# Merging the preparation products of a DeltaNet recurrence into the recurrence's own visits of TensorE

## The chip, the cores and the metric

The kernel runs on one core of a Trainium2 chip. The metric is device time in microseconds (us); the time of a kernel is the median of several executions. A profile shows one execution, with the engines named PE (TensorE's matmuls), PEld (TensorE's weight loads), DVE (VectorE), ACT (ScalarE), POOL (GpSimd) and SP (SyncE, which here only issues DMAs).

## The reference

Two blocks follow each other, in float32. The first is a DeltaNet layer over 4 batches, 8 heads, 768 positions and head dimension 48:

```
k_n = k / (norm(k) + 1e-06)
for t in range(S):
    y[t]  = q[t] @ state
    v_old = state^T k_n[t]
    state = state + beta[t] * outer(k_n[t], v[t] - v_old)
```

The second takes y as 3072 tokens of width 384 (8 heads x 48) through a gated FFN of width 1536:

```
out = (silu(x @ w_gate) * (x @ w_val)) @ w_out
```

## The kernel before

**Chunks.** The sequence is cut into 12 chunks of 64 positions. A chunk of all 32 batch-heads gives 256 tokens, which are one unit of the FFN. The FFN of chunk c (called FFN c here) carries the recurrence of chunk c+1 inside it.

**The FFN.** `gate_val` (L840) computes two of the twelve 128-wide slices of the hidden layer: the gate product, then the value product (`p_gate` and `p_val`, L847), each in one bank of a four-bank rotation in PSUM that `ps_ffn` (L74) hands out. ACT applies Silu, and DVE multiplies into `h_f` (L862). Six such gate pairs make an FFN. From FFN 3 on `output_fast` (L950) does the second product with seven small products per 2x2 split instead of eight; for this the last three gate pairs also form sums of h on DVE (`sums_of_h`, L942), and the output adds up on DVE (L969).

**The recurrence.** `advance(c)` (L730) is a generator of four steps: first v minus what the state predicts (`p_r`, and with it `p_y`, the state's share of y); then `p_u`, which applies the chunk's inverse `zt`; then the new state (`p_s`) and the rest of y (`p_y`, L782); then the transposes (`p_f`, L827) that make `x_ffn`, the input of the next FFN. Its products are 64x64, 32 of them in a group.

**What a chunk needs beforehand.** `turned` (L410) turns k and q of a chunk. From chunk 6 (k) and 3 (q) on it is one DVE instruction each (L422) out of blocks that were loaded by eight DMAs, and it issues the loads of the next chunk's blocks on SP. `gram` (L470) makes the k-k and the q-k products (L444); DVE copies the first (L467) and masks the second (L459). For each pair of chunks, `invert(g)` (L641) solves for the inverse on DVE: turns, a square root by a power on POOL (L655), then 31 steps of two instructions each (`substitute`, L505), and turns again. `join(g)` (L696) then completes the inverse with two groups of 32x32 products on TensorE (L706 and L720), with ACT between them.

**The order of the work.** All five engines' queues are filled in the order of the program text. Two helpers spread the recurrence over the FFN. `point(c+1)` (L1091) stands at nine places of an FFN from FFN 3 on: before each of the six gate pairs, before the output, and twice in it (L984 and L991). Such a place is called a visit here, numbered 0 to 8; the word is also used for the group of small products that TensorE then does between the FFN's products. A point does one thing: the next step of `advance` if it has begun; else one piece of preparation, by `prep_step` (L1064): half a join, or `turned`, or both Gram products of `products` (L1029); else the first step of `advance`. `finish` (L1099) at an FFN's end does what is left. `fill(n)` (L1110) puts the next n pieces of the inverse on DVE: two and three in each gate pair, then 2, 2 and 7 in the output, the 7 at its end (L1003). Where a piece waits for POOL, it says so and the fill is cut short.

**PSUM.** Eight banks: four for the FFN, and two pairs with the tags `px` and `py`, which the recurrence and its preparation share. A tile of a tag waits until the one before it in that tag has been read.

Of the kernel before, what the change touches and what calls it, by code (L numbers as in the profile page):

```python
# [11 lines left out]
ALU = mybir.AluOpType  # L12
# [9 lines left out]
def kernel(  # L22
# [25 lines left out]
    nc = tc.nc  # L48
# [21 lines left out]
    def ps_pair(name, tag):  # L70

        return psum.tile([128, 2, 512], FP32, name=name, tag=tag, bufs=1)

    def ps_ffn(shape, name):  # L74
        return psum.tile(shape, FP32, name=name, tag="ffn", bufs=4)
# [261 lines left out]
    def every():  # L337
        for bp in range(NB):
            for j in range(NJ):
                for n, (par, b) in enumerate(ORDER):  # L340
                    yield bp, j, par, b, bp == 0 and j == 0
# [128 lines left out]
    def gram(*args):  # L470
        for _ in gram_steps(*args):
            pass
# [100 lines left out]
    def recur(p, m=D):  # L573
        p = p[:, :, 0 : NB * NJ * m]
        return p.rearrange("p x (bp j d) -> p x bp j d", bp=NB, j=NJ)
# [120 lines left out]
    def join(g):  # L696

        zt, a, z1 = ztp[g % ZB], a_sb[g], z1s[g]
        M = HH // 2
        p_j = ps_pair("p_j", "px")[:, 0].rearrange("p (c m i) -> p c m i", c=2, m=M)  # L700
        for c in range(2):
            for m in range(M):
                for e in range(2):
                    for s in range(2):
                        dst, lo = QUADS[2 * s + e][0], QUADS[2 * s + 1][0]
                        nc.tensor.matmul(  # L706
                            p_j[dst, c, m],
                            a[lo, c, 2 * m + e, 0:R],
                            zt[lo, c, 2 * m + e, R:C],
                        )  # L710
        t2 = work.tile([128, 2, M, R], FP32, name="t2", tag="tmp", bufs=1)
        nc.scalar.mul(t2, p_j, -1.0)
        yield
        p_j = ps_pair("p_j", "py").rearrange("p e (c m i) -> p e c m i", c=2, m=M)
        for c in range(2):
            for m in range(M):
                for e in range(2):
                    for s in range(2):
                        row, hi = QUADS[2 * s + e][0], QUADS[2 * s][0]
                        nc.tensor.matmul(p_j[hi, e, c, m], z1[row, c, m], t2[row, c, m])  # L720
        zt_v = zt.rearrange("p c (m e) i -> p e c m i", e=2)
        for s, copy in ((0, nc.scalar.copy), (1, nc.vector.tensor_copy)):
            hi = QUADS[2 * s][0]
            copy(
                zt_v[hi, :, :, :, R:C].rearrange("p e c m i -> p e (c m) i"),
                p_j[hi].rearrange("p e c m i -> p e (c m) i"),
            )
        yield

    def advance(c):  # L730

        kn = knp[slot(c)]
        zt = ztp[c // 2 % ZB][:, c % 2]
        zt = zt.rearrange("p (par bp j) i -> p par bp j i", par=2, bp=NB)
        if c > 0:
            scale_v(c)
        r = vin.pop(c)
        p_y = recur(ps_pair("p_y", "py"))
        if c > 0:
            p_r = recur(ps_pair("p_r", "px"))  # L740
            for bp, j, par, b, first in every():
                nc.tensor.matmul(  # L742
                    p_r[half_of(b ^ par), par, bp, j],
                    kt[c][half_of(par), bp, j, b],
                    state[half_of(par), b, bp, j],
                    start=first,
                    stop=True,
                    skip_group_check=True,
                )
            for bp, j, par, b, first in every():  # L750
                nc.tensor.matmul(  # L751
                    p_y[half_of(b ^ par), par, bp, j],
                    qt[c][half_of(par), bp, j, b],
                    state[half_of(par), b, bp, j],
                    start=first,
                    stop=False,
                    skip_group_check=True,
                )
            nc.vector.tensor_tensor(out=r, in0=r, in1=p_r, op=ALU.subtract)  # L759
        yield  # L760
        p_u = recur(ps_pair("p_u", "px"))
        for bp, j, par, b, first in every():
            nc.tensor.matmul(  # L763
                p_u[half_of(b), par, bp, j],
                zt[half_of(b ^ par), par, bp, j],
                r[half_of(b ^ par), par, bp, j],
                start=first,
                stop=True,
                skip_group_check=True,
            )  # L770
        uu = work.tile([128, 2, NB, NJ, D], FP32, name="uu", tag="r", bufs=2)
        each = range(NB) if c == 0 else (slice(0, NB),)
        for bp in each:
            nc.scalar.copy(uu[:, :, bp], p_u[:, :, bp])
        if c + 2 < NCH:
            load_v(c + 2)
        yield
        pq = p_sb.pop(c)

        def p_of_u():  # L780
            for bp, j, par, b, first in every():
                nc.tensor.matmul(  # L782
                    p_y[half_of(b ^ par), par, bp, j],
                    pq[half_of(b), par, bp, j],
                    uu[half_of(b), par, bp, j],
                    start=(c == 0 and first),
                    stop=True,
                    skip_group_check=True,
                )

        def of_state():
            p_s = recur(ps_pair("p_s", "px"))
            for bp, j, par, b, first in every():
                nc.tensor.matmul(  # L794
                    p_s[half_of(par), b, bp, j],
                    kn[half_of(b), bp, 2 * j + par],
                    uu[half_of(b), par, bp, j],
                    start=first,
                    stop=True,
                    skip_group_check=True,  # L800
                )
            if c > 0:
                nc.vector.tensor_tensor(out=state, in0=state, in1=p_s, op=ALU.add)
            else:
                nc.scalar.copy(state, p_s)
            for later in range(AHEAD, NCH):
                if freed_by_k(later) == c:
                    load_k(later)

        if 0 < c < NCH - 1:  # L810
            of_state()
        p_of_u()
        y = work.tile([128, NB, NJ, 2, D], FP32, name="y", tag="r", bufs=2)
        for bp in each:
            nc.scalar.copy(y[:, bp, :, 0], p_y[:, 0, bp])
            for b in range(2):
                nc.scalar.copy(y[half_of(b), bp, :, 1], p_y[half_of(1 - b), 1, bp])
        yield

        y_f = y.rearrange("p bp j par d -> p bp (j par d)")  # L820
        xts[c] = ffn_pool.tile([128, KT, TOK], FP32, name="x_ffn")
        p_f = ps_pair("p_f", "py")[:, :, 0 : KT * 128]
        p_f = p_f.rearrange("p bp (t n) -> p t bp n", t=KT)
        for bp in range(NB):
            for t in range(KT):
                at = slice(t * 128, (t + 1) * 128)
                nc.tensor.transpose(p_f[:, t, bp], y_f[:, bp, at], ident)  # L827
        x_v = xts[c].rearrange("p t (bp n) -> p t bp n", bp=NB)
        for bp in each:
            nc.scalar.copy(x_v[:, :, bp], p_f[:, :, bp])  # L830
        yield
        if c == 0:
            of_state()
            yield
# [181 lines left out]
    def step(kind, fn, *args):  # L1016
        key = (kind, args or (1,))
        if key not in gens:
            gens[key] = [fn(*args), 0]
        next(gens[key][0], None)  # L1020
        gens[key][1] += 1

    def steps(kind, *args):
        return gens.get((kind, args), (None, 0))[1]

    fills = []
# [32 lines left out]
    def may_advance(c):  # L1059
        g = c // 2  # L1060
        due = {0: 1, 1: 2 + 2 * (c % 2)}.get(g, 2)
        return steps("advance", c) > 0 or (c in p_sb and steps("join", g) >= due)

    def prep_step(c):  # L1064
# [23 lines left out]
        going.append(gen)  # L1088
        return True

    def point(c):  # L1091

        mine = c < NCH and steps("advance", c) < 4 and may_advance(c)
        if mine and steps("advance", c) > 0:
            step("advance", advance, c)
        elif not prep_step(c - 1) and mine:
            step("advance", advance, c)

    def finish(c):  # L1099

        if c < NCH:
            while not may_advance(c):
                fill_some(1000)
                prep_step(c - 1)
            while steps("advance", c) < 4:
                step("advance", advance, c)
# [190 lines left out]
```

## Time and profile before

| what | value |
|---|---|
| median of 8 runs | 738.55 us (738.05 to 740.39) |
| profiled execution, its own time | 738.55 us |
| span of the profile | 736.8 us |
| PE busy | 699.2 us, 95% |
| DVE busy | 473.1 us, 64% |
| ACT, POOL busy | 154.7 and 67.8 us |

TensorE's first products of each FFN start at these times; a visit that stands before gate pair 0 is counted to its FFN:

| FFN | 3 | 4 | 5 | 6 | 7 | 8 | 9 | 10 | 11 |
|---|---|---|---|---|---|---|---|---|---|
| start, us | 249.63 | 304.83 | 361.88 | 415.88 | 472.93 | 526.93 | 582.53 | 636.54 | 687.88 |
| busy DVE, us | 24.2 | 46.7 | 27.9 | 46.7 | 27.8 | 44.4 | 26.9 | 13.8 | 11.1 |

The inverse of a pair of chunks runs mostly in the FFNs 4, 6 and 8, and ends in the one after.

How to read the profile's lines: a row of the order of time gives the start, the length, the engine, the line of the program, the operation, the tile written and those read, the count of merged instructions, and in brackets how long the engine had been idle and what released it. A float32 matmul leaves two records, so a gate product of six matmuls is x12, and a group of 32 small products is x64. Records of matmuls overlap, since they are pipelined; the distance between starts is what TensorE takes. A row of the waits gives who waited for whom: us in total, times, the longest.

### The profile page before, as it was taken

What the parts mean: (1) busy time and instruction counts of PE and PEld (TensorE: products, weight loads), DVE (VectorE), ACT (ScalarE), POOL (GpSimd) and SP (SyncE); (2) the same over time, 40 slices, a digit from 0 to 9 for tenths busy, and PEclk for the clock granted to TensorE, in tenths of its full rate; (3) what the DMA queues carried; (4) which work ended last, traced back from release to release, by engine and by line L of the source; (5) the groups of instructions that cost most, each with busy time, mean ns of one, the idle gap of its engine ahead of it and who ended that gap; (6) DMA issues with size and microseconds to landing.
All of it is one profiled execution on the core that took longest, in us unless ns stands there. A gap on an engine that the chain in (4) does not pass through costs nothing.

```text
span 736.8 us, 22478 instructions
## 1 busy us (share of the span) xinstructions
PE 699.2 (95%) x10132; PEld 605.8 (82%) x10132; DVE 473.1 (64%) x977; ACT 154.7 (21%) x287; POOL 67.8 (9%) x46
## 2 busy tenths in 40 slices
PE   4657999999999999999999999999999999999997
PEld 3545788866787788988988988988988988989987
DVE  6999988888498163678853678854678853313122
ACT  3555443302401112021012011012011012021010
POOL 7009100202100000030000030000030000000000
PEclk9957999999999999999999999999999999999999
DMA  7775343221231112330302331302211100100000
GB/s 147 185 227 150 114 109 129 40 37 24 57 45 24 23 24 45 44 67 12 54 3 46 43 64 21 51 3 41 45 28 14 31 3 3 23 3 0 22 1 21
DMA packets 130735, 37.18 MB, mean 50 GB/s; under 512 B 122864, under 2 KB 125936, under 8 KB 130640
## 3 DMA queue, kind: packets, MB, share of 16 engines
q1 hardware_dynamic: 127184, 34.01, 22.4%
q10 hardware_dynamic: 3072, 1.57, 1.0%
q8 instruction: 79, 1.29, 0.7%
q0 software_dynamic: 384, 0.17, 0.1%
q14 instruction: 16, 0.13, 0.1%
HBM read 31.01 MB, written 4.72 MB: 48 GB/s over the span
## 4 chain that ended last, share of the span: by engine, by line
PE 80%; DVE 15%; issue 2%; DMA 1%; ACT 1%; SPq 0%; DVEq 0%; ACTq 0%
PE p_gate L847 24%; PE p_val L847 23%; PE p_o L959 14%; PE p_o L876 6%; DVE tmp L510 3%; DVE zb L516 3%; PE p_g L444 2%; PE p_u L763 2%; PE p_r L742 1%; PE p_s L794 1%; PE p_y L782 1%; PE p_y L751 1%; DVE h_f L917 1%; DVE h_f L862 1%; PE p_j L630 1%
## 5 line engine op out<-in xcount | busy, mean ns | idle before, releaser
L847 PE MATMUL p_gate<-x_ffn,wg_sb 128*128 128x256 f32 x864 | 206.3, 389 | 1.5 <-ACT x_ffn L830 1.5
L847 PE MATMUL p_val<-x_ffn,wv_sb 128*128 128x256 f32 x864 | 198.5, 379 | 0.0
L847 PEld LDWEIGHTS p_gate<-x_ffn,wg_sb 128*128 128x128 f32 x864 | 162.4, 193 | 24.8 <-ACT x_ffn L830 2.0
L847 PEld LDWEIGHTS p_val<-x_ffn,wv_sb 128*128 128x128 f32 x864 | 163.8, 190 | 22.3
L862 DVE TENSOR_TENSOR h_f<-sil,p_val 128x512 f32<-128x512 f32 x71 | 48.6, 684 | 147.7 <-PE p_val L847 147.1
L856 ACT ACTIVATE sil<-p_gate 128x512 f32<-128x512 f32 x72 | 43.0, 598 | 278.4 <-PE p_gate L847 252.6
L655 POOL TENSOR_TENSOR n_b<-mb,half 128x32 f32<-128x32 f32 x5 | 43.9, 8772 | 407.7 <-DVE mb L480 368.2
L959 PE MATMUL p_o<-wo_sb,h_f 128*128 128x192 f32 x432 | 75.6, 328 | 0.1
L959 PEld LDWEIGHTS p_o<-wo_sb,h_f 128*128 128x128 f32 x432 | 70.3, 190 | 1.2 <-DVE o_sb L969 0.7
L510 DVE TENSOR_TENSOR tmp<-zb,mb 128x31 f32<-128x31 f32 (+15 forms) x186 | 63.3, 340 | 12.1 <-PE p_j L630 6.8
L516 DVE TENSOR_TENSOR zb<-zb,tmp 128x31 f32<-128x31 f32 (+15 forms) x186 | 63.7, 343 | 6.6 <-DVE tmp L510 0.2
L969 DVE TENSOR_TENSOR o_sb<-o_sb,p_o 128x192 f32<-128x192 f32 x45 | 15.7, 350 | 53.4 <-PE p_o L959 36.2
L876 PE MATMUL p_o<-wo_sb,h_f 128*128 128x384 f32 x136 | 45.7, 490 | 0.0
L876 PEld LDWEIGHTS p_o<-wo_sb,h_f 128*128 128x128 f32 x136 | 25.4, 190 | 16.5
L959 PE MATMUL p_o<-last_k,h_f 128*128 128x192 f32 x180 | 32.2, 326 | 0.0
L959 PEld LDWEIGHTS p_o<-last_k,h_f 128*128 128x128 f32 x180 | 29.7, 190 | 0.0
L917 DVE TENSOR_TENSOR h_f<-h_f,h_f 128x256 f32<-128x256 f32 x54 | 22.4, 424 | 8.0 <-PE p_o L959 7.1
L959 PE MATMUL p_o<-last_h,h_f 128*128 128x192 f32 x144 | 26.3, 326 | 0.0
L959 PEld LDWEIGHTS p_o<-last_h,h_f 128*128 128x128 f32 x144 | 23.9, 190 | 0.0
L254 ACT ACTIVATE last_h<-last_h,rebias 128x512 int32<-128x512 uint32 (+2 forms) x26 | 15.3, 615 | 28.7 <-DVE last_h L246 28.7
L763 PEld LDWEIGHTS p_u<-vin,zt 64*64 64x64 f32 x768 | 13.7, 141 | 6.4 <-issue 3.2
L763 PE MATMUL p_u<-vin,zt 64*64 64x48 f32 x768 | 15.7, 228 | 1.8 <-DVE vin L759 0.7
(180 smaller groups left out, 691.6 us busy)
## 6 DMA issues: line engine op xcount, KB each, us to landing
vin<-in_v_dram SPq DMA_DIRECT2D x96, 48.0 KB
kn<-in_k_dram SPq DMA_DIRECT2D x40, 96.0 KB
out_dram<-o_sb SPq DMA_DIRECT2D x36, 96.0 KB
zt<-in_moe_w_out_dram SPq DMA_DIRECT2D x6, 384.0 KB
staged<-in_moe_w_out_dram SPq DMA_DIRECT2D x6, 384.0 KB
qpad<-in_q_dram SPq DMA_DIRECT2D x36, 64.0 KB
wo_sb<-in_moe_w_gate_dram SPq DMA_DIRECT2D x4, 512.0 KB
wo_sb<-in_moe_w_val_dram SPq DMA_DIRECT2D x4, 512.0 KB
```

The costliest lines, as they stand in the source:

```text
L254: nc.scalar.activation(power.bitcast(I32), power, ACTF.Relu, bias=rebias, scale=8.0)
L510: nc.vector.tensor_tensor(out=t_v, in0=zb[:, 0 : j + 1, j : j + 1].to_broadcast([128, j + 1, m]), in1=mb[:, j : j + 1, j + 1 : R].to_broad ...
L516: nc.vector.tensor_tensor(out=zb[:, 0 : j + 1, j + 1 : R], in0=zb[:, 0 : j + 1, j + 1 : R], in1=t_v, op=ALU.add,)
L655: nc.gpsimd.tensor_tensor(out=n, in0=mb.rearrange("p j i -> p (j i)")[:, 0 : R * R : R + 1], in1=half, op=ALU.pow,)
L763: nc.tensor.matmul(p_u[half_of(b), par, bp, j], zt[half_of(b ^ par), par, bp, j], r[half_of(b ^ par), par, bp, j], start=first, stop=True, ...
L847: nc.tensor.matmul(ps[name][:, i], w_sb[:, t, (f + i) * 128 : (f + i + 1) * 128], xts[c][:, t], start=(t == 0), stop=(t == KT - 1),)
L856: nc.scalar.activation(sil, ps[name], ACTF.Silu)
L862: nc.vector.tensor_tensor(out=hs[c, f], in0=sil, in1=ps["p_val"], op=ALU.mult)
L876: nc.tensor.matmul(p_o, hs[c, f - f % 2][:, f % 2, bp * 128 : (bp + 1) * 128], wo_sb[:, f], start=(f == 0), stop=(f == FT - 1),)
L917: nc.vector.tensor_tensor(out=out, in0=a, in1=b, op=ALU.subtract)
L959: nc.tensor.matmul(p[x, part], a(f - f % 2)[:, f % 2], b(f), start=not begun and f == 0, stop=f == FH - 1, skip_group_check=True,)
L969: nc.vector.tensor_tensor(out=out, in0=a, in1=b, op=ALU.add)
```

## The change

From FFN 3 on (`point(c)` with c > 3) a new function `merged(c)` takes the place of the old rule. It has stages: 0 turns k (if one is free to be turned) and q; 1 does `advance`'s first step and one Gram product (that of k for an odd chunk that has one, else that of q); 2 does, for an even chunk, the first half of the join and the k Gram, and waits (doing nothing) until a visit earlier than its own has seen the inverse as ended; for an odd chunk with a k Gram it does the q Gram, and an odd chunk without one skips it; 3, for even chunks, does the second half of the join; 4, 5 and 6 do the other three steps of `advance`. `finish` runs the stages that are left.

In `advance` the product `p_y` of the state moves from the first step to the second, ahead of `p_u`; this holds for the chunks 1 to 3 too. In `join` the first `p_j` takes a bank of the FFN's rotation in place of the pair `px`.

```diff
@@ join
-        p_j = ps_pair("p_j", "px")[:, 0].rearrange("p (c m i) -> p c m i", c=2, m=M)
+        p_j = ps_ffn([128, 512], "p_j").rearrange("p (c m i) -> p c m i", c=2, m=M)
@@ advance
-        p_y = recur(ps_pair("p_y", "py"))
         if c > 0:
             p_r = recur(ps_pair("p_r", "px"))
             for bp, j, par, b, first in every():
...
+            nc.vector.tensor_tensor(out=r, in0=r, in1=p_r, op=ALU.subtract)
+        yield
+        p_y = recur(ps_pair("p_y", "py"))
+        if c > 0:
             for bp, j, par, b, first in every():
                 nc.tensor.matmul(
                     p_y[half_of(b ^ par), par, bp, j],
...
-            nc.vector.tensor_tensor(out=r, in0=r, in1=p_r, op=ALU.subtract)
-        yield
         p_u = recur(ps_pair("p_u", "px"))
@@ new
+    stage_of, seen = {}, set()
+
+    def merged(c):
+        if c >= NCH:
+            return
+        at, k_c, q_c = stage_of.get(c, (0, None, None))
+        g = c // 2
+        ready = c % 2 == 1 or g in seen
+        seen.update(inverted)
+
+        def a_step():
+            step("advance", advance, c)
+
+        def gram_k(tag):
+            if k_c is not None:
+                gram(k_c, False, tag, (nc.vector.tensor_copy,) * 2)
+                if k_c % 2 == 1:
+                    fills.append((k_c // 2, invert(k_c // 2)))
+
+        if at == 0:
+            if going:
+                next(going.pop())
+                return
+            if k_of and steps("advance", freed_by_k(k_of[0])) >= 4:
+                k_c = k_of.pop(0)
+                turned(k_c, False)
+            if q_of and q_of[0] == c:
+                q_c = q_of.pop(0)
+                turned(q_c, True)
+        elif at == 1:
+            a_step()
+            if c % 2 == 1 and k_c is not None:
+                gram_k("py")
+            else:
+                gram(q_c, True, "py")
+                if c % 2 == 1:
+                    at = 3
+        elif at == 2:
+            if not ready:
+                return
+            if c % 2 == 0:
+                if steps("join", g) < 1:
+                    step("join", join, g)
+                gram_k("px")
+            else:
+                gram(q_c, True, "px")
+                at = 3
+        elif at == 3:
+            if steps("join", g) < 2:
+                step("join", join, g)
+        elif at < 7:
+            a_step()
+        stage_of[c] = (at + 1, k_c, q_c)
@@ point
+        if c > 3:
+            merged(c)
+            return
@@ finish
-        if c < NCH:
+        if c > 3:
+            while c < NCH and steps("advance", c) < 4:
+                if stage_of.get(c, (0,))[0] == 2 and c % 2 == 0 and c // 2 not in inverted:
+                    fill_some(1000)
+                merged(c)
+        elif c < NCH:
```

## The prediction

> **What bounds the kernel now.** I read the page first, then the table of busy time by stretch (one per FFN), then who waits for whom on TensorE from 245 us on, then TensorE's order of time, and last VectorE's around the places where TensorE stands still.
>
> ```profile
> span 736.8 us, 22478 instructions
> PE 699.2 (95%) x10132; PEld 605.8 (82%) x10132; DVE 473.1 (64%) x977; ACT 154.7 (21%) x287; POOL 67.8 (9%) x46
> PE 80%; DVE 15%; issue 2%; DMA 1%; ACT 1%; SPq 0%; DVEq 0%; ACTq 0%
> 304.80:361.90 57.10, 56.05 (x812) 50.36 (x812) 46.67 (x96) 7.25 (x13) 7.34 (x3) 1.00 0.33 49
> 361.90:415.90 54.00, 54.00 (x815) 48.39 (x814) 27.85 (x50) 8.85 (x15) 0.00 (x0) 1.00 0.13 25
> ...
> PE p_g L444 <- DVE kt L422: 1.9, 2, 1.0
> PE p_g L444 <- DVE qt L422: 1.0, 1, 1.0
> ```
>
> The columns of the stretches are length, then busy time of PE, PEld, DVE, ACT, POOL, then clock and DMA. From chunk 3's FFN on TensorE is never idle but for three stalls, 2.9 us in all, each a Gram product waiting for a VectorE transpose. The time is TensorE's work plus its stalls.
>
> ```profile
> 637.63 2.86 PE L847 MATMUL p_gate<-x_ffn,wg_sb 128*128 128x256 f32 x12
> 643.00 1.15 PE L742 MATMUL p_r<-state,kt 64*64 64x48 f32 x64
> 643.97 1.11 PE L751 MATMUL p_y<-state,qt 64*64 64x48 f32 x64
> 645.02 2.86 PE L847 MATMUL p_gate<-x_ffn,wg_sb 128*128 128x256 f32 x12
> 650.39 1.15 PE L763 MATMUL p_u<-vin,zt 64*64 64x48 f32 x64
> 651.47 2.86 PE L847 MATMUL p_gate<-x_ffn,wg_sb 128*128 128x256 f32 x12
> 663.87 2.75 PE L847 MATMUL p_gate<-x_ffn,wg_sb 128*128 128x256 f32 x12
> 669.05 2.75 PE L847 MATMUL p_gate<-x_ffn,wg_sb 128*128 128x256 f32 x12
> ```
>
> From the start of one gate product to the next: 5.18 us with no visit between (663.87 to 669.05), 6.45 with a visit of one group of 64x64 products, 7.39 with two. So one group costs 1.27, the second in the same visit 0.94, and opening a visit 0.33.
>
> **The change: visits saved.** I count visits from FFN 3 to FFN 10 (FFN c carries the recurrence of chunk c+1). Before: 7, 6, 6, 6, 6, 6, 6, 5 = 48. After: for an even chunk p_r with the q Gram, first join half with the k Gram, second join half, p_y with p_u, p_s with p_y, transposes = 6; for an odd one with a k Gram 5 (the q Gram stands alone); chunk 11 4. That is 6, 5, 6, 5, 6, 5, 6, 4 = 43. No product is added or removed. 5 x 0.33 = **-1.65**. Bounds: two of the merged visits (FFN 5 and 7) put 32x32 products before 64x64 ones. The nearest row is chunk 0's state product followed by a join:
>
> ```profile
> 66.94 1.15 PE L794 MATMUL p_s<-uu,kn 64*64 64x48 f32 x64
> 68.02 0.75 PE L620 MATMUL p_j<-zt,a_sb 32*32 32x32 f32 x64
> ```
>
> 1.08 us apart against 0.97 within one size (643.00 to 643.97), so 0.11 more each; at worst the whole 0.33 is lost twice: -1.65 to -0.99. I keep -1.65, with the 0.22 as its likely error. [...]
>
> **Stalls removed.** Before, `turned` is put behind gate pair 4's VectorE work in FFN 4, 6 and 8, and the Gram follows one gate pair later:
>
> ```profile
> 344.20 1.25 DVE L422 STREAM_TRANSPOSE kt<-qpad 128x1024 f32<-128x1024 f32 x1
> 345.37 1.20 DVE L422 STREAM_TRANSPOSE qt<-qpad 128x1024 f32<-128x1024 f32 x1
> 345.50 1.16 PE L444 MATMUL p_g<-kt 64*64 64x64 f32 x64 [0.95 <-DVE kt L422]
> 346.72 1.16 PE L444 MATMUL p_g<-qt,kt 64*64 64x64 f32 x64
> ```
>
> From that gate's start (339.21) to the output's first product (347.81) is 8.60 us; the same place without a stall (393.99 to 401.37) takes 7.38. So 1.22 in FFN 4, 1.22 in FFN 6 (450.26 to 458.86), and in FFN 8 (561.31 to 568.78, one group) 7.47 - 6.45 = 1.02: **-3.46**. In FFN 4 and 6 the last output product also waits 0.21 for VectorE's late sums (358.96 to 359.82 against 0.65 at 579.93 to 580.58): **-0.42**. Both go if nothing is late in their place.
>
> **Stalls added.** What is late next is the q Gram at visit 1 of an even chunk (FFN 5, 7, 9). Visits are counted 0 to 5 before the six gate pairs, 6 before the output, 7 and 8 in it. `turned` stands at visit 0, in VectorE's queue behind the last output's `fill(7)`. An inverse is 45 calls of `fills`: 3 turns, 2 waits for POOL, 2 for norms and scaling, 31 steps, 6 more turns and the end. Before, it starts behind visit 0 of FFN 4: 4 calls in pair 0 (cut by the wait), 1 + 3, then 5 in each of four pairs (28), 2 + 2 + 7 in the output (39), 5 and 1 in FFN 5's pairs 0 and 1. So the join comes at visit 2, where the trace has it (372.33, two gate pairs after 361.88). After, it starts behind visit 1, five calls later, so `fill(7)` holds steps 21 to 27 rather than 26 to 31. In VectorE's order behind FFN 5's start at 361.88:
>
> ```profile
> 361.88 2.75 PE L847 MATMUL p_gate<-x_ffn,wg_sb 128*128 128x256 f32 x12
> 362.08 0.35 DVE L969 TENSOR_TENSOR o_sb<-o_sb,p_o 128x192 f32<-128x192 f32 x1 [1.91 <-PE p_o L959]
> 362.35 0.31 DVE L510 TENSOR_TENSOR tmp<-zb,mb 128x156 f32<-128x156 f32 x1
> 362.70 0.32 DVE L516 TENSOR_TENSOR zb<-zb,tmp 128x156 f32<-128x156 f32 x1
> ```
>
> The last sum waits for the output's end, the first step starts 0.47 after the FFN does. Steps 21 to 27 have 231, 220, 207, 192, 175, 156 and 135 columns; by the starts of the same forms they take 0.87 + 0.84 + 0.82 + 0.76 + 0.74 + 0.70 + 0.60 = 5.33. Then the k transpose (1.17 to the next start) and the q transpose (1.20) end at 0.47 + 5.33 + 1.17 + 1.20 = 8.17, and a Gram started 0.15 after its transpose (346.57 to 346.72): 8.32. TensorE reaches it at 5.27 (a gate pair up to a visit, 361.88 to 367.06 plus 0.09) + 0.97 (p_r) = 6.24. Stall 2.08 in FFN 5 and 7. FFN 9 has no k left: 0.47 + 5.33 + 1.25 + 0.14 = 7.19, stall 0.95. Sum **+5.11**. Bounds: nothing, as in FFN 4, 6, 8, where VectorE idles at the boundary; at most, every step at the 0.93 of the largest form (128x256), 3.3 + 3.3 + 2.1 = +8.7. I take 5.11 since every term is a row of the same form. Behind the waiting Gram stand the next gate pair, its Silu on ACT and its h_f; all move by the stall.
>
> On the clock: the table shows 1.00 in the stretch that holds a 0.95 stall, so I price these stalls without a slower restart. [...]
>
> **Edits costed at nothing, with their cover.** *p_y moved to p_u's visit* (chunks 1 to 3 too): same groups, one visit shorter, the next longer; p_u comes no earlier and its subtract was queued no later (chunk 1's p_u already waits 0.70 for it). *p_j in the FFN's four banks*: it takes the bank of a gate product two pairs back, long read by ACT. *p_s and p_y at visit 7, transposes at 8 for even chunks*: between them 24 output products, 3.9 us; the y copies take 0.48 + 0.96. Behind the transposes 24 more products cover x_ffn's copy (0.80). *SP*: `turned`'s 16 block loads (5.2 + 4.8 us of issue) go behind four stores; they are needed one FFN later, some 50 us. *POOL*: the pow (6.21) starts one pair later and VectorE waits some 2.7 us rather than 1.3; walking its queue on, h_f of pair 3 ends 1.4 us late and pair 4 is on time. *VectorE in FFN 5*: h_f of pair 1 ends at 20.7 after the start (8.2 transposes, 1.2 steps, 0.7 h_f, 1.0 steps, 1.9 turn, 3.2 recurrence, 3.9 turns, 0.7), and the bank is wanted at 22.4: 1.7 us of cover. If that is gone, every further us costs one, three times.
>
> **The sum.** -1.65 - 3.46 - 0.42 + 5.11 = -0.42. The profiled execution took 738.55 (span 736.8 and 1.75 around it), which is also the median of the eight: **738.1**. About 0.2% (1.5 us) is what a measurement of this kernel can tell from no change, so this is "no difference". Its own range is 736.5 to 739.7 (0.33 twice, 0.3 on each stall).
>
> **Rivals.** *Nine visits are not enough* (slower). An even chunk needs 7 visits and idles at 2 and 3: its inverse ends with call 45 in pair 2, visit 3 only notes it, the join comes at 4 and the transposes at 8, the last. Four calls of slack are left in pair 2; from a fifth on, the transposes fall behind the output and the next FFN waits for x_ffn. The row: transposes at 407.33, x_ffn ends at 408.98, a product could go at 407.98; 1.1 us three times: 741.4, and some 745 if two visits fall out. Against it: the count meets the trace of before. *VectorE is further behind than walked* (slower): the 1.7 us cover goes, or the output's sums come late again; 1 to 2 us three times, 741 to 744. For it: 46.7 of 57.1 us busy in such a stretch. *VectorE is ahead* (faster): steps or transposes are past when visit 1 comes. With no stall -5.53: 733.0; half, 735.6. Against it: `fill(7)` stands ahead of `turned`. *No gain from merging*: +1.65, 739.8.
>
> **How the numbers follow.** The forecast has 0.55 (0.45 inside 0.2%, 0.08 faster, 0.02 slower), VectorE ahead 0.18, too few visits 0.12, VectorE behind 0.13, no merging gain 0.02. Faster 0.26, same 0.45, slower 0.29. Leaving 0.1 out below and 0.1 above, the range is 735.0 to 742.0.
>
> **What would show it.** Right: no stall in FFN 4, 6, 8; TensorE idle some 2.1 us before the q Gram at visit 1 of FFN 5 and 7 and 1 us in FFN 9, released by the q transpose; joins at visit 4; p_f the last visit of FFN 5, 7, 9. Wrong: p_f behind the last output product, a gate product waiting for h_f, or no wait at visit 1.

## The result and the profile after

The changed kernel takes 743.07 us (median of 12, 741.29 to 745.11), the kernel before 738.55. The ratio is 1.0057, with a 95% interval of 1.0048 to 1.0065: slower by half a per cent, beyond the 0.2% that a measurement can tell. The forecast was 738.1 with a range of 735.0 to 742.0; the time lies 1.1 us above the range.

The profiled execution took 743.57 us. Its page, then its stretches, one per FFN from FFN 3 on (length, busy time of PE, PEld, DVE, ACT and POOL, TensorE's clock, DMA):

```profile
span 741.8 us, 22467 instructions
PE 699.8 (94%) x10132; PEld 608.3 (82%) x10132; DVE 474.5 (64%) x977; ACT 154.7 (21%) x287; POOL 65.4 (9%) x46
```

```profile
304.70:358.00 53.30, 53.30 (x684) 48.17 (x683) 40.92 (x82) 7.25 (x13) 6.58 (x3) 1.00 0.24 39
358.00:417.70 59.70, 57.74 (x940) 51.97 (x940) 34.04 (x64) 8.85 (x15) 0.00 (x0) 0.97 0.21 35
417.70:471.00 53.30, 53.30 (x684) 48.17 (x683) 41.00 (x82) 7.25 (x13) 6.58 (x3) 1.00 0.24 39
471.00:532.60 61.60, 57.91 (x940) 51.99 (x940) 34.04 (x64) 8.85 (x15) 0.00 (x0) 0.97 0.21 34
532.60:585.90 53.30, 53.30 (x684) 48.17 (x683) 41.05 (x82) 7.25 (x13) 6.58 (x3) 1.00 0.14 24
585.90:641.80 55.90, 55.06 (x876) 49.59 (x875) 31.65 (x61) 8.85 (x15) 0.00 (x0) 1.00 0.10 16
```

FFN 4, 6 and 8 (53.3 us) have no stall left and are as short as forecast: six bare gate pairs and an output are 44.73 (687.88 to 718.96 and 674.23 to 687.88 before), the five visits 8.66 (three of two groups at 2.21, one of one group at 1.27, the transposes at 0.76, by rows of before). FFN 5 and 7 are the ones to look at. They do the same work (x940), yet take 59.7 and 61.6 us, and both have a clock of 0.97. What TensorE waits for from 245 us on:

```profile
PE p_g L444 <- DVE qt L422: 4.7, 3, 2.0
PE p_g L444 <- issue: 1.7, 1, 1.7
```

The first line is the stall that the forecast placed there, three times. TensorE's order of time shows it in FFN 5:

```profile
357.99 2.75 PE L848 MATMUL p_gate<-x_ffn,wg_sb 128*128 128x256 f32 x12
363.26 1.15 PE L741 MATMUL p_r<-state,kt 64*64 64x48 f32 x64
366.36 1.99 PE L444 MATMUL p_g<-qt,kt 64*64 64x64 f32 x64 [1.96 <-DVE qt L422]
368.28 3.59 PE L848 MATMUL p_gate<-x_ffn,wg_sb 128*128 128x256 f32 x12
374.30 2.75 PE L848 MATMUL p_gate<-x_ffn,wg_sb 128*128 128x256 f32 x12
```

The Gram starts 8.37 after the FFN (8.32 forecast) and waits 1.96 (2.08). But behind the wait everything is slow: the Gram's 64 records take 1.92 to the next start, where such a group takes 1.09, and the gate product is 3.59 long, not 2.86. The stretches around it give the reason:

```profile
362.00:364.00 2.00, 2.00 (x56) 1.56 (x57) 1.76 (x7) 0.00 (x0) 0.00 (x0) 1.00 0.00 0
364.00:366.00 2.00, 0.41 (x28) 0.28 (x20) 2.00 (x2) 0.00 (x0) 0.00 (x0) 1.00 0.03 8
366.00:368.00 2.00, 1.64 (x60) 1.64 (x64) 1.90 (x7) 0.00 (x0) 0.00 (x0) 0.60 0.63 84
368.00:370.00 2.00, 2.00 (x21) 1.59 (x14) 1.86 (x5) 0.00 (x0) 0.00 (x0) 0.55 0.70 91
370.00:372.00 2.00, 2.00 (x11) 1.77 (x10) 1.90 (x3) 0.09 (x1) 0.00 (x0) 1.00 0.71 92
```

The granted clock falls to one half as the stall ends and comes back some 3.4 us later. I call this a halving below. In FFN 7 the Gram's stall (1.95) passes without one, but there is something else, in the visit that joins the inverse and does the k Gram:

```profile
490.90 2.75 PE L848 MATMUL p_gate<-x_ffn,wg_sb 128*128 128x256 f32 x12
496.18 1.29 PE L706 MATMUL p_j<-zt,a_sb 32*32 32x32 f32 x128
497.39 0.62 PE L444 MATMUL p_g<-kt 64*64 64x64 f32 x25
499.75 1.34 PE L444 MATMUL p_g<-kt 64*64 64x64 f32 x39 [1.74 <-issue]
501.02 3.78 PE L848 MATMUL p_gate<-x_ffn,wg_sb 128*128 128x256 f32 x12
508.54 0.70 PE L848 MATMUL p_gate<-x_ffn,wg_sb 128*128 128x256 f32 x2
```

TensorE pauses for 1.74 us in the middle of a group, with nothing in the profile that it waits for, and then runs at half clock again. From gate product to the second next one this is 17.64 us (490.90 to 508.54); the same place in FFN 5 takes 14.17 (379.48 to 393.65). Of the 3.47 more, 1.74 are the pause; the other 1.73 I put down to the halving.

### The profile page after: what moved, and what is told of

Read it like the earlier page. It is cut to its first block, busy times and chain, and to the rows that moved or that the text cites. A ratio compares the mean times of both kernels' runs of the same rounds, so it can differ in the third digit from the quotient of the medians.

```text
span 741.8 us, 22467 instructions
## 1 busy us (share of the span) xinstructions
PE 699.8 (94%) x10132; PEld 608.3 (82%) x10132; DVE 474.5 (64%) x977; ACT 154.7 (21%) x287; POOL 65.4 (9%) x46
## 3 DMA queue, kind: packets, MB, share of 16 engines
q8 instruction: 79, 1.29, 0.7%
## 4 chain that ended last, share of the span: by engine, by line
PE 84%; DVE 12%; issue 2%; DMA 1%; ACT 0%; SPq 0%; DVEq 0%; ACTq 0%
PE p_gate L848 24%; PE p_val L848 23%; PE p_o L960 17%; PE p_o L877 6%; PE p_g L444 3%; DVE tmp L510 2%; DVE zb L516 2%; PE p_y L754 1%; PE p_s L795 1%; PE p_u L764 1%; PE p_y L783 1%; PE p_r L741 1%; PE p_f L828 1%; DVE last_h L287 1%; DMA kn<-in_k_dram 1%
## 5 line engine op out<-in xcount | busy, mean ns | idle before, releaser
L655 POOL TENSOR_TENSOR n_b<-mb,half 128x32 f32<-128x32 f32 x5 | 41.6, 8313 | 420.4 <-DVE mb L480 380.6
L444 PE MATMUL p_g<-qt,kt 64*64 64x64 f32 x704 | 14.3, 237 | 4.7 <-DVE qt L422 4.7
L444 PEld LDWEIGHTS p_g<-qt,kt 64*64 64x64 f32 x704 | 12.8, 150 | 6.8 <-DVE qt L422 5.1
```

What stands on the lines that cost most here:

```text
L444: nc.tensor.matmul(p_v[par][half_of(b if of_q else b ^ par), bp, j], kt[c][half_of(par), bp, j, b], xt[half_of(par), bp, j, b],)
L655: nc.gpsimd.tensor_tensor(out=n, in0=mb.rearrange("p j i -> p (j i)")[:, 0 : R * R : R + 1], in1=half, op=ALU.pow,)
```

## The experiments

The leading theory was that two things lie on top of the forecast's sum, halvings that fall by chance and the pause. The rivals: VectorE's lateness costs by itself, the merged visits cost by themselves, and the pause is chance.

**The changed kernel once more.**

> The changed kernel once more, unaltered. The sum on record missed by some 5 us, and in the trace all of it lies in two places: FFN 5 (59.7 us for 57.9 expected) with the clock at 0.5 behind the stall of 1.96, and FFN 7 (61.6 for 57.9) with a pause of 1.74 inside the k Gram of the merged join visit, released by nothing that the profile shows, and the clock at 0.5 behind it. Theory (clock): the halvings fall by chance, each costs some 1.8 us, so the times stand in steps of 1.8 (741.5, 743.2, 745.0) and this profile may show them at other stalls. If the pause belongs to the program it is there again in FFN 7; if it is chance it is gone or elsewhere. Rival (VectorE is late): the same places every time, whatever the clock. About 743.1 by both.

742.69 us (741.58 to 744.31), ratio 1.0056 (1.0044 to 1.0069). The pause is in FFN 7 again (1.73), in the middle of the same group, so it belongs to the program. The halvings moved: this time behind both stalls of FFN 5 and 7, and none behind the pause.

**q turned before k.**

```diff
+            even = c % 2 == 0
+            if even and q_of and q_of[0] == c:
+                q_c = q_of.pop(0)
+                turned(q_c, True)
             if k_of and steps("advance", freed_by_k(k_of[0])) >= 4:
                 k_c = k_of.pop(0)
                 turned(k_c, False)
-            if q_of and q_of[0] == c:
+            if not even and q_of and q_of[0] == c:
```

> For even chunks q is turned before k, so that the q Gram at visit 1 waits for one transpose fewer: the stall falls from 2.0 to about 0.85 in FFN 5 and 7 and stays 0.85 in FFN 9. Stall alone: -2.3, 740.8. Clock theory: the halvings behind these two stalls go as well, some 0.8 of them per run at 1.8 each, so 739.3 to 740.0. If VectorE's lateness as a whole is what costs, no more than the 2.3.

739.84 us, ratio to the kernel before 1.0010 (0.9999 to 1.0022). The stalls are 0.83, as expected, and the gain is 3.2 us, more than the 2.3 of the stalls. The twelve times stand in steps: four at 737.6 to 737.8, four at 739.2 to 740.1, four at 740.8 to 741.4. The profiled one, 737.62, has the pause (1.87) but no halving. This speaks for the clock theory and against a price of VectorE's lateness alone.

**The k Gram away from the join's visit.**

```diff
+    idle = []
...
             if not ready:
+                idle.append(c)
+                if c % 2 == 0 and k_c is not None and idle.count(c) == 2:
+                    gram_k("px")
+                    stage_of[c] = (2, None, q_c)
                 return
```

> For even chunks the k Gram leaves the join's visit and stands alone at visit 3, which is idle. It costs two visits more: +0.66. If the pause of 1.74 in FFN 7 comes of the long burst of small products in one visit (128 joins and 64 Gram records with as many weight loads), it goes, and the halving behind it: -1.74 - 1.8 + 0.66, so 740.2. If the pause has nothing to do with the merging, 743.7.

741.09 us, ratio 1.0033 (1.0021 to 1.0045). All that TensorE waits for from 245 us on in this kernel:

```profile
PE p_g L444 <- DVE qt L422: 4.8, 3, 2.0
```

The pause is gone with the merged visit. The gain is 2.0 rather than the 2.9 expected: the two stalls of 2.0 are still there, and halvings behind them are more frequent than I had assumed (see the count below). This kernel also gives the price of a halving in FFN 5, where it had none behind the same stall (1.97): from FFN 5's first gate product to its third it takes 14.76 us (357.48 to 372.24), the changed kernel 16.31 (357.99 to 374.30). By this one pair of profiles a halving costs 1.55 there.

**The wait filled with useless products.**

```diff
+    def spin(n):
+        p_d = ps_ffn([128, 512], "p_d")
+        for _ in range(n):
+            nc.tensor.matmul(p_d[:, 0:128], wg_sb[:, 0, 0:128], wg_sb[:, 0, 128:256])
+        nc.scalar.copy(spare, p_d[:, 0:1])
...
             a_step()
+            if c % 2 == 0 and c > 4:
+                spin(9 if c < 10 else 4)
```

> TensorE's wait at visit 1 of FFN 5, 7 and 9 is filled with products that nothing uses (nine of 128x128 by 128 columns, four in FFN 9, into a bank of the FFN's rotation, about 0.22 us each). Nothing is taken from the wait itself: the q Gram still starts when its transpose ends. Clock theory: TensorE is no longer idle there, the halving behind these stalls goes, and a kernel with more work is faster: 741.3 to 742. If idleness is not the cause: 743.1 or a little more.

738.78 us, ratio 1.0010 (1.0001 to 1.0019). More work made the kernel 4.3 us faster, where 1 to 2 were expected.

```profile
363.76 1.15 PE L741 MATMUL p_r<-state,kt 64*64 64x48 f32 x64
364.84 2.27 PE L1097 MATMUL p_d<-wg_sb 128*128 128x128 f32 x18
367.04 1.16 PE L444 MATMUL p_g<-qt,kt 64*64 64x64 f32 x64
```

The Gram starts 8.55 after the FFN (358.49), later than with the stall; only the idleness is gone, and the halvings with it. The rest of the gain I put down to the pause: it is not in this trace either, though the join's visit is still merged. That was a surprise, and the next idea came from it: the added products push TensorE's later instructions along its stream.

**A longer stall.**

```diff
+    def again(c):
+        xt = kts[slot(c)]
+        nc.vector.tensor_copy(xt, xt)
...
                 turned(k_c, False)
+                if c % 2 == 0:
+                    again(k_c)
```

> VectorE copies the turned k onto itself once more between the k and the q transpose of an even chunk (128x1024, some 1.2 us), so the stall at visit 1 of FFN 5 and 7 goes from 2.0 to some 3.2; FFN 9, without a k, stays at 0.85. The wait alone: +2.4, 745.3. Clock theory: with a longer stall the clock halves behind it more surely (both times in nearly every run, where it was 0.8 times of 2), so 746.5 to 748, and the steps in the times become rarer.

745.47 us, ratio 1.0092 (1.0070 to 1.0114), below what was expected. The copy took less than I had put (the stall grew to 2.72, not 3.2), and in the profiled execution only one of the two stalls was followed by a halving. So a longer stall in this range does not make the halving certain.

**Transposes a visit earlier, ahead of the fill of 7.**

```diff
         elif at < 7:
             a_step()
+        elif at == 9 and c % 2 == 1 and c > 4 and c + 1 < NCH:
+            merged(c + 1)
```

> The transposes of an even chunk move from visit 0 of its FFN to visit 8 of the FFN before (idle there), ahead of the fill of 7, and the first step with the q Gram to visit 0. No stall is left at the q Gram, no halving behind it, and the five saved visits stay. By the terms on record 738.55 - 5.53 = 733.0 without the pause in the merged join visit; with it and a halving behind it 736.5. If VectorE's output sums come late through the transposes, some 0.5 more at three places.

736.25 us, ratio 0.9965 (0.9952 to 0.9978). No stall is left at the q Gram. The pause is there, with a halving behind it in the profiled execution; the case "with it" had been put at 736.5.

**The same, with the k Gram alone.**

> As the kernel with early transposes, with the k Gram of even chunks alone at an idle visit: two more visits (0.66), and no burst of join and k Gram in one visit. 733.0 + 0.66 = 733.7. Where the pause had gone from the other one already, that one is the faster by 0.66; where not, this one by about 3.

733.79 us, ratio 0.9939 (0.9923 to 0.9955): this one is faster than the kernel before and than the one with early transposes. TensorE is never idle from 300 to 700 us in it; two of the stretches:

```profile
350.00:400.00 50.00, 50.00 (x786) 44.66 (x785) 34.84 (x69) 6.62 (x11) 0.00 (x0) 1.00 0.17 27
400.00:450.00 50.00, 50.00 (x785) 45.01 (x784) 31.19 (x56) 8.55 (x15) 6.58 (x3) 1.00 0.35 56
```

The sum of the terms on record without the added stalls, plus two visits, was 733.7. So the saved visits and the removed stalls were priced right, taken together.

**Both Gram products of even chunks alone.**

```diff
-            else:
+            elif c % 2 == 1 or c == 4:
                 gram(q_c, True, "py")
...
+            if c % 2 == 0 and q_c is not None and c > 4:
+                gram(q_c, True, "py")
+                stage_of[c] = (2, k_c, None)
+                return
             if not ready:
+                if c % 2 == 0 and k_c is not None:
+                    gram_k("px")
+                    stage_of[c] = (2, None, q_c)
                 return
```

> For even chunks the q Gram goes to visit 2 and the k Gram to visit 3, both idle, so nothing is merged but p_y with p_u (and the Gram of odd chunks and of chunk 4). Transposes stay at visit 0, behind the fill of 7. The stall goes because the q Gram comes one gate pair later (11.7 us behind the FFN's start, transposes end at 8.2). Three and two visits more: +1.65. 733.0 + 1.65 = 734.7, clearly faster than before if the stalls, the pause and the clock are all that cost.

735.18 us, ratio 0.9950 (0.9938 to 0.9962), near the 734.7. Here the transposes stand where the change put them, just as late; what is gone is TensorE waiting for them. For a price of VectorE's lateness alone that leaves at most the 0.5 us between the two numbers.

**Where the pause comes from.** I counted all of TensorE's records ahead of each pause from FFN 3 on. These are the matmuls and the weight loads, and also the 75 records of its sequencer (waits for semaphores and drains); 62 of those stand ahead of 14529, and without them the counts have no common remainder (14467 is 131 modulo 256).

```
kernel                    pause in           records ahead   modulo 256
changed (both profiles)   FFN 7, k Gram      14529           193
q turned first            FFN 7, k Gram      14529           193
longer stall              FFN 7, k Gram      14529           193
early transposes          FFN 7, k Gram      14529           193
```

All of them fall on the same place by necessity, since these kernels give TensorE the same stream up to there. The pauses of the start-up stand at 193 modulo 256 too (449, 961, 1217 and 1473 in the kernel before). The changed kernel's page has 79 transfers of 16 KB on its queue `q8 instruction` (1.29 MB), called blocks here, and 20339 records of TensorE over 79 blocks are 257 for each. Around the pause of the changed kernel, in the 0.7 us ahead of it, the DMA view shows one such transfer:

```profile
DMA packets 1, 0.02 MB, mean 23 GB/s; under 512 B 0, under 2 KB 0, under 8 KB 0
q8 instruction: 1, 0.02, 9.5%
```

The pause ends 1.38 us after this block has landed (498.37). So it is for all seven pauses from FFN 3 on, in six profiles: the transfer starts 0.67 to 1.06 us ahead of the pause, and TensorE goes on 1.28 to 1.52 us after the landing. No other block from 245 us on, in any of the 13 traces, was begun less than 1.67 us after it had landed.

The merged join and k Gram are 64 + 32 products, each two matmuls and two weight loads: 384 instructions in 2.3 us. The theory, that TensorE waits there for a block, then predicts where a pause falls if the stream is shifted, which two kernels tried: 16 and 40 products of 32x32 (64 and 160 instructions) at visit 1 of FFN 3, on top of the early transposes.

```diff
+    def shift(n):
+        p_d = ps_ffn([128, 512], "p_d")
+        quad = slice(0, R)
+        for j in range(n):
+            at = slice(R * (j % 4), R * (j % 4) + R)
+            nc.tensor.matmul(p_d[at, 0:R], ident[quad, quad], ident[quad, quad])
+        nc.scalar.copy(spare, p_d[:, 0:1])
...
             a_step()
+            if c == 4:
+                shift(16)
```

> Kernel with early transposes, and 16 small products (32x32, used by nothing) at visit 1 of FFN 3, which push all later TensorE instructions 64 places down its stream. Theory (instruction fetch): every pause released by nothing in the traces so far stands where the count of TensorE's matmul and weight-load records is 193 modulo 256, and one block of 16 KB arrives per 256 instructions. The merged join and k Gram are 384 instructions; in FFN 7 they begin at 141 modulo 256, so they meet such a place after 52 and again after 308, too fast for the next block. Pushed by 64 they begin at 205 (FFN 7) and 32 (FFN 5): one such place within the 384, no pause, no halving behind it. 736.25 - 1.97 - some 1.0 + 0.4 for the added products: 733.5 to 734. Rival (the pause belongs to this visit, or to this k): still in FFN 7, 736.6.

733.89 us, ratio 0.9933 (0.9921 to 0.9945). From 250 to 700 us TensorE never waits:

```profile
250.00:700.00 450.00, 450.00 (x6336) 406.27 (x6335) 260.62 (x500) 66.33 (x116) 19.75 (x9) 1.00 0.17 28
```

The useless products that filled the waits were such a shift too: 72 records ahead of FFN 7's visit, which then begins at 213 and meets one such place.

> The same with 40 products: all later instructions pushed by 160. The visit in FFN 7 begins at 45 and meets one such place, that in FFN 5 begins at 128 and meets two, after 65 and 321. By the fetch theory the pause moves from FFN 7 to FFN 5, at the k Gram's first third, and the time is as with early transposes plus the added products (0.9): 736 to 737. Rival: pause in FFN 7 still, or none.

740.97 us, ratio 1.0023 (1.0011 to 1.0035). The time missed, by 4 us; the place did not. The pause left FFN 7 and stands in FFN 5, behind the 32nd record of the k Gram, which is 321 instructions into the visit:

```profile
385.75 1.29 PE L706 MATMUL p_j<-zt,a_sb 32*32 32x32 f32 x128
386.96 0.69 PE L444 MATMUL p_g<-kt 64*64 64x64 f32 x32
389.28 0.69 PE L444 MATMUL p_g<-kt 64*64 64x64 f32 x32 [1.62 <-issue]
389.90 4.54 PE L848 MATMUL p_gate<-x_ffn,wg_sb 128*128 128x256 f32 x12
```

What I had overlooked is that the 40 products themselves make the visit in FFN 3 one of 416 instructions, with two such places in it. It has a pause too, at record 7873, again 193 modulo 256, and both pauses were followed by a halving:

```profile
256.63 0.89 PE L1099 MATMUL p_d<-ident 32*32 32x32 f32 x80
257.44 1.16 PE L444 MATMUL p_g<-qt,kt 64*64 64x64 f32 x63
259.95 0.27 PE L444 MATMUL p_g<-qt,kt 64*64 64x64 f32 x1 [1.35 <-issue]
260.15 4.11 PE L848 MATMUL p_gate<-x_ffn,wg_sb 128*128 128x256 f32 x10
```

So the remainder held in a place that I had not thought of. Two places in one visit are not enough by themselves, though. The second join of FFN 3 has 256 instructions, and in the changed kernel with 16 products, the next one, it passes two places 1.59 us apart (268.16 and 269.75) without a wait: there the block's transfer had started at 266.90, ahead of the first place, and not behind it as in the pauses (496.38 and 497.30 in the changed kernel). The same 16 products in the changed kernel, its stalls left:

> The changed kernel with the same 16 products at visit 1 of FFN 3, its stalls left alone. The pause of 1.74 goes, and the halving behind it where there was one: 743.07 - 1.74 - 0.7 + 0.4 = 741.0. What is left above 738.1 are halvings behind the two stalls of 2.0 (some 1.2 per run at 1.9, as they were in the kernel with the k Gram alone). Rival: 743.4.

740.44 us, ratio 1.0017 (1.0006 to 1.0029): the pause is gone and 2.6 us with it. What remains above 738 are the halvings behind the two stalls; the profiled execution, 741.37, has both.

**How often a wait halves the clock.** Over the nine profiles that have a wait on TensorE from FFN 3 on, the kernel before included, 17 waits are 1.35 us or longer; a halving follows 11 of them. 11 waits are 0.83 to 1.04 us; none is followed by one. The changed kernel has three of the long kind, so by this share some 1.9 halvings per run. One, two and three would fit its times (741.3 to 742.0, 743.0 to 743.6, 744.9 and 745.1), but no trace shows it for the runs without a profile, and the kernel before, whose profile has no halving there, scatters from 737.7 to 740.6 too.

Within an execution the place of a halving is not chance. In each of the 13 traces all changes of the clock lie whole multiples of 3.413 us apart, and where this grid begins differs from one execution to the next: from 245 us on the falls of the changed kernel start at 366.39 and 499.51 (39 times 3.413 apart), the first in its second profile at about 367.4. These are stretches of the grid around the changed kernel's three long waits:

```profile
362.98:366.39 3.41, 1.45 (x70) 1.05 (x68) 3.27 (x6) 0.00 (x0) 0.00 (x0) 1.00 0.05 10
366.39:369.81 3.42, 3.42 (x68) 3.03 (x69) 3.18 (x10) 0.00 (x0) 0.00 (x0) 0.50 0.69 91
475.62:479.03 3.41, 1.78 (x68) 1.30 (x66) 3.23 (x6) 0.00 (x0) 0.00 (x0) 1.00 0.00 0
479.03:482.45 3.42, 3.10 (x73) 2.83 (x74) 3.18 (x11) 0.00 (x0) 0.00 (x0) 1.00 0.61 82
496.10:499.51 3.41, 1.91 (x154) 1.71 (x154) 1.88 (x4) 0.60 (x1) 0.00 (x0) 1.00 0.02 5
499.51:502.93 3.42, 3.18 (x44) 2.70 (x44) 1.29 (x2) 0.00 (x0) 0.00 (x0) 0.50 0.02 5
```

The stall of FFN 5 lies in one stretch (1.96 us idle), and the next one runs at half clock. That of FFN 7 is cut by a line of the grid (1.63 and 0.32), and nothing follows. The pause has 1.50 in one stretch, and a halving follows. From 245 to 700 us all 11 halvings fill the stretch behind one that holds 1.35 to 2.47 us of idle time; the six long waits without a halving were each cut by a line, the longer stall of FFN 7 (2.72) into 1.48 and 1.23. (Three of the waits with one were cut too, but left 1.50 to 2.47 in one stretch.) Idle time is not all that counts: three stretches with 1.39, 1.48 and 1.63 us of it were followed by none. By the distance of starts they hold 0.64 to 1.28 us of the FFN's 128x128 products, the 11 at most 0.33. Ahead of FFN 3 even these two figures do not separate the cases: three kernels have a stretch near 87 us with 1.66 idle, only small products and no halving behind it, and the kernel before has one halving behind 0.97. What decides between them was not shown.

## Why the prediction was wrong

The order of the visits, the place of the stalls and their size were right, and so was the saving; the time of the whole was not, because two prices were put at nothing: the clock behind the added stalls, and a pause in the merged visit.

- *Visits saved (-1.65).* Right within what the runs tell. The 43 visits stand where the text put them, p_f last in FFN 5, 7 and 9, and the joins at visit 4. The merged join and k Gram cost 2.40 (379.48 to 387.06, less 5.18) where 1.31 + 0.94 = 2.25 had been taken; 0.15 each for the row's 0.11.
- *Stalls removed (-3.46 - 0.42).* Right: FFN 4, 6 and 8 have none.
- *Stalls added (+5.11).* Right: 1.96, 1.95 and 0.84 of idle time for 2.08, 2.08 and 0.95. VectorE's queue went as walked; the k transpose started 5.95 after the FFN (5.80).
- *The clock.* This step failed: "so I price these stalls without a slower restart". It rested on a stretch that held a 0.95 stall at a clock of 1.00, and carried that over to stalls of 2. The part of the trace of before that was read, from 245 us on, has no fall of the clock; the part ahead of it has (one case stands below the list). Over the runs 11 of the 17 waits of 1.35 to 2.72 us, between or within groups of small products, were followed by a halving. In the changed kernel the clock was 0.50 for 3.41 us both times (366.39 to 369.81 and 499.51 to 502.93), at 1.55 and, by what was left over, 1.73 us.
- *The merged join and k Gram.* The pause of 1.74 us is a term that the text did not have at all. It priced the merging by the switch between 32x32 and 64x64 products, and no row of the join's or Gram's own visits from 245 us on showed a pause inside a visit.

The trace of before holds a case of each term ahead of 245 us. In its start-up TensorE pauses with nothing to wait for, at 193 modulo 256 as well, once in a group of L444 (at 31.43 us); and the clock falls for one stretch behind another with only 0.97 us of idle time and mostly small products:

```profile
PE p_g L444 <- issue: 1.8, 1, 1.8
```

```profile
72.84:76.25 3.41, 2.44 (x126) 2.26 (x127) 3.41 (x9) 2.36 (x5) 2.94 (x1) 1.00 0.85 226
76.25:79.67 3.42, 3.42 (x10) 2.71 (x9) 3.42 (x8) 2.69 (x5) 0.00 (x0) 0.50 0.93 253
```

Together: 738.1 + 1.74 + 1.55 + 1.73 = 743.1 for the profiled execution, which took 743.57; the 0.4 left are small terms: the joins' 0.3 and a start of FFN 3 that is 0.18 later (249.81 for 249.63) on one side, stalls that are 0.36 shorter than priced on the other, and the rest is not traced. Of the rivals, none was this one. "Nine visits are not enough" and "VectorE is further behind than walked" name the same side and a near time for reasons that the trace does not have: the transposes p_f stand at visit 8, and no gate product waits for an h_f.

## What to carry to other kernels

When TensorE has to wait, count what the wait does to its clock: a wait of 2 us between groups of small products cost up to 1.7 us again, or nothing, by how it lay in a grid of 3.41 us that begins elsewhere in each execution. Merging small products into one visit saves its opening (0.33 us here) but visits of 384 and 416 instructions paused 1.35 to 1.97 us where two block places fell in them. That TensorE waits there for its instructions is my reading; no trace names what released it. Where the visit begins in the stream counted: pushed on by 64 records it had no pause (740.44 for 743.07 us), so an edit elsewhere can bring or take one. A transposing step that feeds TensorE belongs ahead of the filler work in VectorE's queue, not behind it: with that and the k Gram left alone, the same idea gave 733.79 us (0.9939, 0.9923 to 0.9955).

## What the runs showed of the hardware

- Useless products in a wait made a kernel faster: 738.78 for 743.07 us. Part of that is the halvings avoided, part the pause, which the same products shifted away; the two parts were not measured apart in that kernel. With the pause alone shifted away the time was 740.44 us.
- The changed kernel has one instruction block of 16 KB for 257 of TensorE's records, and the visits of 384 and 416 instructions that passed two block places (193 modulo 256 by the records) within 1.6 to 1.9 us paused 1.35 to 1.97 us, seven times of seven. TensorE went on 1.28 to 1.52 us after the block had landed. What sets the start of a block's transfer was not shown.
- Whether a wait is followed by a halving is not a matter of its length alone: 2.72 us passed without one, 1.35 us did not. In the 13 traces the clock changes on a grid of 3.413 us, and all six long waits without a halving were cut by a line of it. What else decides was not shown: three stretches with 1.39, 1.48 and 1.63 us of idle time were followed by no halving, the 11 that were hold 1.35 to 2.47.
